# Gated linear recurrence into a gated MLP: squares, magnitude cap and scaled v made a group ahead, weights loaded in nine pieces

## The chip, the cores and the metric

One core of one Trainium2 chip runs the whole kernel. The metric is the device time of one execution in microseconds (us), as the median of several runs. TensorE is called PE below, VectorE DVE, ScalarE ACT, GpSimd POOL and SyncE SP.

## The reference, cut to what matters

Attention with a decaying complex state (batch 4, 8 heads, 768 steps, head size 48), then a gated MLP over 3072 tokens (384 to 1536 and back):

```python
mag = np.sqrt(a_re * a_re + a_im * a_im)
scale = np.minimum(mag, 0.999) / (mag + 1e-06)
a_re_n, a_im_n = (a_re * scale, a_im * scale)
for t in range(S):
    new_re = ar * S_re - ai * S_im
    new_im = ar * S_im + ai * S_re
    S_re, S_im = (new_re + k_t[:, None] * v_t[None, :], new_im)
    y[:, :, t] = einsum('bhd,bhde->bhe', q[:, :, t], S_re)
...
gate = 1.0 / (1.0 + np.exp(-(x @ w_gate)))
val = x @ w_val
return (gate * val @ w_out)
```

## The kernel before, in words

The 3072 tokens are 24 slabs of 128 (4 batches of 6 chunks). Slabs are gathered in ten groups of 1, 2, 3, 3, 3, 3, 3, 3, 2, 1 slabs, numbered 0 to 9. The recurrence is done in chunks: the logarithm of the magnitude and the phase of `a` are summed along the 128 steps by matmuls with triangular matrices, q and k are scaled and turned by the results, and a masked score matrix plus a carried state gives y.

For a group g these pieces exist:

- `loads_a(g)` and `loads_q(g)` issue on SP the loads of a_re and a_im (tile `a2`, 2 buffers) and of q, k (tile `qk`, 2 buffers) and v (tile `v32`, 1 buffer).
- `prep_a(g)`: ACT loads a table set with Ln and Exp, squares `a2` into `sq` (L162). POOL adds the two squares into `lm` (L165) and caps it (L167), slab by slab. ACT takes Ln of a_re (L170) and Exp of its negative (L171), both in place, then Ln of `lm` (L173). POOL multiplies a_im by 1/a_re (L175). Then for each slab PE sums `lm` (tile `cl`, L182), ACT makes exp(+cl/2) and exp(-cl/2) (tile `ee`, L183 and L185), SP sends the last row through DRAM (`scr`, `rbe`), POOL multiplies q and k by `ee` (L197) and makes the scaled 16-bit copy `v16` of v (L199).
- `prep_b(g)`: ACT loads a table set, takes Arctan of `a2` (L209), loads a third set (L210). For each slab PE sums the phase (tile `ct`, L215, L218, L231), POOL keeps the running phase (`run`, L223, L225), DVE rounds (L229), ACT takes Abs and two Sines (L235 to L238), DVE writes the turned k and q (`kst`, `qst`, L242).
- `attn(g)`: transposes (L292, L293), carried state (L268, L274, L278, L282), scores (L304), mask (L308), y (L319, L321), its copy by ACT (L324) and transpose (L331).
- `gateval(g)`: 12 blocks of the MLP's gate and value products on PE (L362, L367), Tanh on ACT (L370), the product on DVE (L371). Four PSUM buffers serve this and the output product.
- `outproj(g)`: the output product on PE (L381), a copy on ACT (L387) and the store.

The pieces are generators, and iteration i of the main loop has two halves. The first half merges the first two fifths of attn(i), outproj(i-2) and prep_a(i+1); the second merges the rest of attn(i), gateval(i-1) and prep_b(i+1). `merge` takes always the generator whose next step has the smallest share (step number divided by its count of steps). ACT runs its instructions in exactly this written order. PE, DVE, POOL and SP get their orders from a planner, which goes by program order among the instructions that its own model holds ready; each engine then runs its queue in order. A tile's next write waits until the old readers of its buffer are done.

The weights are loaded by 18 transfers on POOL's queue with a cast to 16 bit (6 of 128 rows by 1536 for gate and value, 12 of 128 by 384 for the output), issued behind the first group's L175.

Of the kernel before, what the change touches and what calls it, by code (L numbers as in the profile page):

```python
# [9 lines left out]
FT = mybir.ActivationFunctionType  # L10
ALU = mybir.AluOpType
# [6 lines left out]
YSC = 2.0**10  # L18
# [4 lines left out]
def kernel(  # L23
# [12 lines left out]
    nc = tc.nc  # L36
# [5 lines left out]
    DFF = moe_w_gate.shape[1]  # L42
    NFB = DFF // 128
# [5 lines left out]
    GROUPS = [SLABS[f:f + n] for f, n in zip(FIRST, SIZES)]  # L49
    NG = len(GROUPS)  # L50
# [41 lines left out]
    gs = [Grp() for _ in range(NG)]  # L92

    def loads_a(g):
        G = gs[g]
        G.a2 = pa.tile([L, 2, NS, HD], F32, name=f"a2_{g}", tag="a2")
        for s, (b, c) in enumerate(GROUPS[g]):
            for i, src in enumerate((a_re, a_im)):
                nc.sync.dma_start(
                    G.a2[:, i, s].rearrange("t (h d) -> t h d", d=D),  # L100
                    src[b, :, c * L:(c + 1) * L].rearrange("h t d -> t h d"))

    def loads_q(g):
        G = gs[g]
        G.qk = pq.tile([L, 2, NS, HD], F32, name=f"qk_{g}", tag="qk")
        G.v32 = pv_.tile([L, NS, HD], F32, name=f"v32_{g}", tag="v32", bufs=1)
        G.v16 = pv_.tile([L, NS, HD], F16, name=f"v16_{g}", tag="v16")
        for s, (b, c) in enumerate(GROUPS[g]):
            for dst, src in ((G.qk[:, 0, s], q), (G.qk[:, 1, s], k),
                             (G.v32[:, s], v)):  # L110
                nc.sync.dma_start(
                    dst.rearrange("t (h d) -> t h d", d=D),
                    src[b, :, c * L:(c + 1) * L].rearrange("h t d -> t h d"))
# [21 lines left out]
    wg16 = const.tile([128, 3, DFF], F16, name="wg16")  # L135
    wv16 = const.tile([128, 3, DFF], F16, name="wv16")
    wo16 = const.tile([128, NFB, DM], F16, name="wo16")

    def load_weights():
        for j in range(3):  # L140
            nc.gpsimd.dma_start(wg16[:, j], moe_w_gate[j * 128:(j + 1) * 128])
            nc.gpsimd.dma_start(wv16[:, j], moe_w_val[j * 128:(j + 1) * 128])
        for j in range(NFB):
            nc.gpsimd.dma_start(wo16[:, j], moe_w_out[j * 128:(j + 1) * 128])

    rbe, arr = {}, {}
    for b in range(B):
# [3 lines left out]
    scr = [dram.tile([NCH, HD], F32, name=f"scr{b}", bufs=1, tag=f"scr{b}")  # L151
           for b in range(B)]

    def prep_a(g):
        G = gs[g]
        n = len(GROUPS[g])
        ar, ai = G.a2[:, 0, :n], G.a2[:, 1, :n]
        G.lm = pa.tile([L, NS, HD], F32, name=f"lm_{g}", tag="lm")
        sq = pa.tile([L, 2, NS, HD], F32, name=f"sq_{g}", tag="sq", bufs=1)
        lm = G.lm[:, :n]  # L160
        nc.scalar.preload_act_table_set("natural_log_exp_and_others")  # L161
        nc.scalar.activation(out=sq[:, :, :n], in_=G.a2[:, :, :n],  # L162
                             func=FT.Square)
        for s in range(n):
            nc.gpsimd.tensor_tensor(out=G.lm[:, s], in0=sq[:, 0, s],  # L165
                                    in1=sq[:, 1, s], op=ALU.add)
            nc.gpsimd.tensor_scalar(out=G.lm[:, s], in0=G.lm[:, s],  # L167
                                    scalar1=CAP, scalar2=-1.0,
                                    op0=ALU.min, op1=ALU.max)
        nc.scalar.activation(out=ar, in_=ar, func=FT.Ln)  # L170
        nc.scalar.activation(out=ar, in_=ar, func=FT.Exp, scale=-1.0)  # L171
        yield
        nc.scalar.activation(out=lm, in_=lm, func=FT.Ln)  # L173
        for s in range(n):
            G.last_pool = nc.gpsimd.tensor_tensor(  # L175
                out=G.a2[:, 1, s], in0=G.a2[:, 1, s], in1=G.a2[:, 0, s],
                op=ALU.mult)
        yield
        for s, (b, c) in enumerate(GROUPS[g]):
            ee = pe_.tile([L, 2, HD], F32, name=f"ee_{g}_{s}", tag="ee")  # L180
            cl = ps_gen.tile([L, HD], F32, name=f"cl_{g}_{s}", tag="gen")
            nc.tensor.matmul(cl, wl_t, G.lm[:, s], start=True, stop=True)  # L182
            nc.scalar.activation(out=ee[:, 0], in_=cl, func=FT.Exp,  # L183
                                 scale=0.5)
            nc.scalar.activation(out=ee[:, 1], in_=cl, func=FT.Exp,  # L185
                                 scale=-0.5)
            nc.sync.dma_start(scr[b][c:c + 1], ee[L - 1:L, 0])
            with nc.allow_non_contiguous_dma(reason="column of decays"):
                for p0 in (0, 64):
                    nc.sync.dma_start(  # L190
                        rbe[b][p0:p0 + D, c],
                        scr[b][c].rearrange("(h d) -> d h", d=D))
            if c > 0:
                nc.vector.tensor_tensor(
                    out=arr[b][:, c - 1], in0=rbe[b][:, c - 1],
                    in1=rbe[b][:, c], op=ALU.mult)
            nc.gpsimd.tensor_tensor(out=G.qk[:, :, s], in0=G.qk[:, :, s],  # L197
                                    in1=ee, op=ALU.mult)
            nc.gpsimd.tensor_scalar(out=G.v16[:, s], in0=G.v32[:, s],  # L199
                                    scalar1=YSC, scalar2=1.0,  # L200
                                    op0=ALU.mult, op1=ALU.mult)
            yield

    def prep_b(g):
# [171 lines left out]
    def outproj(g):  # L376
        G = gs[g]
        for s, (b, c) in enumerate(GROUPS[g]):
            po = ps_moe.tile([128, DM], F32, name=f"po{g}_{s}", tag="moe")
            for fb in range(NFB):  # L380
                nc.tensor.matmul(po, G.p[:, fb, s * L:(s + 1) * L],  # L381
                                 wo16[:, fb], start=(fb == 0),
                                 stop=(fb == NFB - 1))
                if fb % 4 == 3 and fb < NFB - 1:
                    yield
            ot = pmoe.tile([128, DM], F32, name=f"ot{g}_{s}", tag="ot")
            nc.scalar.activation(out=ot, in_=po, func=FT.Copy, scale=0.5)  # L387
            nc.sync.dma_start(out[b * S + c * L:b * S + (c + 1) * L], ot)
            yield

    def merge(*streams):
        live = [[it, 0, n] for it, n in streams]
        while live:
            live.sort(key=lambda x: (x[1] + 1) / x[2])
            x = live[0]
            try:
                next(x[0])
                x[1] += 1
            except StopIteration:
                live.pop(0)  # L400

    def take(it, n):
        for _ in range(n):
            yield next(it)

    def run_all(it):
        for _ in it:
            pass

    def sz(g):  # L410
        return len(GROUPS[g])

    with tc.manual_schedule(engines={ACT}):
        loads_a(1)
        run_all(prep_a(0))
        with tc.issue_after(gs[0].last_pool.ins):
            load_weights()
        loads_q(1)
        run_all(prep_b(0))
        for i in range(NG + 2):  # L420
            st = []
            if i < NG:
                at = attn(i)
                na = 7 * sz(i)
                n1 = na * 2 // 5
                st.append((take(at, n1), n1))
            if 0 <= i - 2:
                st.append((outproj(i - 2), 3 * sz(i - 2)))
            if i + 1 < NG:
                if i + 2 < NG:  # L430
                    loads_a(i + 2)
                st.append((prep_a(i + 1), 2 + sz(i + 1)))
            merge(*st)
            st = []
            if i < NG:
                st.append((at, na - n1))
            if 0 <= i - 1 < NG:
                st.append((gateval(i - 1), 2 * NFB))
            if i + 1 < NG:
                if i + 2 < NG:  # L440
                    loads_q(i + 2)
                st.append((prep_b(i + 1), 1 + 2 * sz(i + 1)))
            merge(*st)
# [1 line left out]
_INS = ['q', 'k', 'v', 'a_re', 'a_im', 'moe_w_gate', 'moe_w_val', 'moe_w_out']  # L445
# [26 lines left out]
```

## Time and profile before

| what | value |
|---|---|
| device time, median of 3 runs | 370.19 us (368.79 to 371.55) |
| device time of the profiled execution | 373.35 us |
| its span, first to last instruction | 371.3 us |
| mean granted TensorE clock | 0.931 |
| PE busy | 277.8 us (75%) |
| PE weight loads | 181.4 us (49%) |
| ACT busy | 224.0 us (60%) |
| DVE busy | 206.1 us (55%) |
| POOL busy | 157.7 us (42%) |

Busy shares are of the span. The profiled execution lies 2.05 us above its span and 3.16 us above the median. No engine is busy all the time; the three rows of ACT, DVE and POOL say nothing of who waits for whom. ACT's load of the Ln and Exp table set (L161) is written once for each group, so its starts mark the iterations: iteration i begins where group i+1's is loaded.

### The profile page before, as it was taken

To read this page: it belongs to the slowest core of one execution; us is meant where nothing else is said; L and a number is where in the kernel's file an instruction comes from. 1 tells how busy PE (TensorE), PEld (TensorE's weight loads), DVE (VectorE), ACT (ScalarE), POOL (GpSimd) and SP (SyncE) were. 2 spreads that over 40 slices of the span, in tenths; PEclk is the share of its full clock that TensorE was granted. 3 is DMA by queue.
4 is the path that set the end of the run, shared out by engine and by line. 5 is a ranking of instruction groups with operands and counts; after the bars stand their busy time and mean duration, and the time that the engine had idled before them with its cause. 6 is when DMAs were issued, how large, how long until landed. Compare 5 with 4: busy or idle time off the path is not lost.

```text
span 371.3 us, 6375 instructions
## 1 busy us (share of the span) xinstructions
PE 277.8 (75%) x2328; PEld 181.4 (49%) x2328; DVE 206.1 (55%) x385; ACT 224.0 (60%) x376; POOL 157.7 (42%) x186
## 2 busy tenths in 40 slices
PE   0310753595569937997889967996799899999996
PEld 0100532364347614664556644663556566666774
DVE  1120281288068905695449725891588489667533
ACT  3604583848385748456774848674956684785343
POOL 3746719723771287026830485028700741320000
PEclk9999995899589968899889989998999999999999
DMA  7999999598166854149240943073202310100101
GB/s 147 199 197 176 185 129 151 71 146 148 33 101 104 147 107 70 39 84 163 56 85 15 187 100 66 3 132 83 44 2 44 102 7 0 51 18 0 65 23 42
DMA packets 150990, 32.70 MB, mean 88 GB/s; under 512 B 145048, under 2 KB 150192, under 8 KB 150960
## 3 DMA queue, kind: packets, MB, share of 16 engines
q1 hardware_dynamic: 148368, 28.76, 44.2%
q0 software_dynamic: 2592, 3.54, 5.3%
q8 instruction: 18, 0.29, 0.3%
q14 instruction: 12, 0.10, 0.1%
HBM read 31.07 MB, written 4.76 MB: 96 GB/s over the span
## 4 chain that ended last, share of the span: by engine, by line
PE 42%; ACT 21%; POOL 11%; DVE 9%; DMA 8%; issue 5%; SPq 3%; ACTq 0%; DVEq 0%; POOLq 0%
PE pg L362 8%; PE cl L182 8%; PE pv L367 7%; POOL lm L165 5%; PE ct L215 4%; PE po L381 3%; ACT sq L162 3%; POOL lm L167 3%; ACT lm L173 3%; DMA wv<-in_moe_w_val_dram 3%; DVE qst L242 2%; PE sc L304 2%; PE ct L218 2%; ACT L161 2%; ACT L208 2%
## 5 line engine op out<-in xcount | busy, mean ns | idle before, releaser
L182 PE MATMUL cl<-lm,wl_t 128*128 128x384 f32 x48 | 30.5, 737 | 60.3 <-ACT lm L173 60.3
L370 ACT ACTIVATE g<-pg 128x384 f16<-128x384 f32 (+2 forms) x120 | 49.5, 427 | 41.8 <-PE pg L362 35.5
L362 PE MATMUL pg<-xt,wg 128*128 128x384 f16 (+2 forms) x360 | 67.6, 296 | 7.6 <-ACT g L370 7.3
L367 PE MATMUL pv<-xt,wv 128*128 128x384 f16 (+2 forms) x360 | 68.8, 295 | 1.9 <-DVE p L371 1.1
L371 DVE SCALAR_TENSOR_TENSOR p<-g,pv 128x384 f16<-128x384 f16 (+2 forms) x120 | 54.8, 468 | 23.8 <-ACT g L370 19.5
L308 DVE TENSOR_TENSOR mst<-sc,msk_t 128x512 f16<-128x512 f32 x48 | 32.4, 682 | 46.3 <-PE sc L304 46.3
L381 PE MATMUL po<-wo,p 128*128 128x384 f16 x288 | 53.6, 326 | 0.0
L296 DVE COPY qkT<-tp 128x1024 f16<-128x1024 f16 x48 | 32.1, 684 | 38.6 <-PE tp L293 38.4
L197 POOL TENSOR_TENSOR qk<-qk,ee 128x768 f32<-128x768 f32 x24 | 44.3, 1859 | 11.9 <-ACT ee L185 11.0
L199 POOL TENSOR_SCALAR v<-v 128x384 f16<-128x384 f32 x24 | 13.4, 560 | 82.8 <-PE y L321 66.7
L165 POOL TENSOR_TENSOR lm<-sq 128x384 f32<-128x384 f32 x24 | 25.8, 1089 | 41.1 <-ACT sq L162 40.6
L362 PEld LDWEIGHTS <-wg 128*128 128x128 f16 x360 | 31.8, 99 | 22.2 <-issue 12.2
L182 PEld LDWEIGHTS cl<-lm,wl_t 128*128 128x128 f32 x48 | 10.5, 265 | 64.4 <-ACT lm L173 63.2
L367 PEld LDWEIGHTS <-wv 128*128 128x128 f16 x360 | 32.4, 98 | 17.9 <-issue 5.9
L215 PE MATMUL ct<-a,wt_t 128*128 128x384 f32 x48 | 25.0, 607 | 12.8 <-ACT a L209 12.8
L229 DVE TENSOR_SCALAR r<-ct 128x384 f16<-128x384 f32 x24 | 13.2, 551 | 37.1 <-PE ct L215 20.2
L381 PEld LDWEIGHTS <-p 128*128 128x128 f16 x288 | 26.3, 98 | 13.7 <-issue 0.2
L292 PE MATMUL tp<-idn_t,kst 128*128 128x128 f16 x192 | 30.6, 236 | 2.8 <-DVE kst L242 2.8
L293 PE MATMUL tp<-idn_t,qst 128*128 128x128 f16 x192 | 30.1, 235 | 1.2 <-DVE qst L242 1.2
L242 DVE TENSOR_TENSOR kst<-qk,cs 128x768 f16<-128x768 f32 x24 | 23.1, 960 | 7.9 <-ACT cs L238 5.4
L162 ACT ACTIVATE sq<-a 128x2304 f32<-128x2304 f32 (+2 forms) x10 | 17.4, 1740 | 14.7 <-DMA a<-in_a_im_dram 14.6
L292 PEld LDWEIGHTS <-kst 128*128 128x128 f16 x192 | 20.3, 107 | 8.1 <-DVE kst L242 4.8
(53 smaller groups left out, 506.1 us busy)
## 6 DMA issues: line engine op xcount, KB each, us to landing
a<-in_a_re_dram SPq DMA_DIRECT2D x24, 192.0 KB, 2.9
a<-in_a_im_dram SPq DMA_DIRECT2D x24, 192.0 KB, 4.2
qk<-in_q_dram SPq DMA_DIRECT2D x24, 192.0 KB, 3.3
qk<-in_k_dram SPq DMA_DIRECT2D x24, 192.0 KB, 3.9
v<-in_v_dram SPq DMA_DIRECT2D x24, 192.0 KB, 2.8
out_dram<-ot SPq DMA_DIRECT2D x24, 192.0 KB
wg<-in_moe_w_gate_dram POOLq DMA_DIRECT2D x3, 384.0 KB, 7.9
wv<-in_moe_w_val_dram POOLq DMA_DIRECT2D x3, 384.0 KB, 7.2
```

The costliest lines, as they stand in the source:

```text
L165: nc.gpsimd.tensor_tensor(out=G.lm[:, s], in0=sq[:, 0, s], in1=sq[:, 1, s], op=ALU.add)
L182: nc.tensor.matmul(cl, wl_t, G.lm[:, s], start=True, stop=True)
L197: nc.gpsimd.tensor_tensor(out=G.qk[:, :, s], in0=G.qk[:, :, s], in1=ee, op=ALU.mult)
L215: nc.tensor.matmul(ct, wt_t, th[:, s], start=True, stop=False, skip_group_check=True)
L292: nc.tensor.transpose(tp[:, 4 + i], G.ks[s][:, h], idn_t)
L296: nc.vector.tensor_copy(out=qkT, in_=tp)
L308: nc.vector.tensor_tensor(out=mst, in0=sc, in1=msk_t.unsqueeze(1).broadcast_to([L, 4, L]), op=ALU.mult)
L362: nc.tensor.matmul(pg, wg16[:, j, fc], G.xt[:, j, :nt], start=(j == 0), stop=(j == 2))
L367: nc.tensor.matmul(pv, wv16[:, j, fc], G.xt[:, j, :nt], start=(j == 0), stop=(j == 2))
L370: nc.scalar.activation(out=g16, in_=pg, func=FT.Tanh, scale=0.5)
L371: nc.vector.scalar_tensor_tensor(out=G.p[:, fb, :nt], in0=g16, scalar=1.0, op0=ALU.add, in1=pv, op1=ALU.mult)
L381: nc.tensor.matmul(po, G.p[:, fb, s * L:(s + 1) * L], wo16[:, fb], start=(fb == 0), stop=(fb == NFB - 1))
```

## The change: what it does, and the diff

Square, the two-square sum, the cap and the scaled copy of v leave prep_a and become a generator of their own, `prep_0`. For group i+2 it is merged into the second half of iteration i, beside attn(i), gateval(i-1) and prep_b(i+1). prep_a(i+1) begins with the table load and then takes Ln of a_re, Ln of `lm` and Exp in that order; it has one step fewer. Both loads of group i+2 stand at the start of iteration i (the loads of q, k and v stood between the halves). Before the main loop prep_0 runs for groups 0 and 1, and both loads of group 1 are written behind prep_a(0). The weights come in 9 transfers: 6 of 512 columns over all 384 rows, 3 of 512 rows of the output weights.

```diff
     def load_weights():
-        for j in range(3):
-            nc.gpsimd.dma_start(wg16[:, j], moe_w_gate[j * 128:(j + 1) * 128])
-            nc.gpsimd.dma_start(wv16[:, j], moe_w_val[j * 128:(j + 1) * 128])
-        for j in range(NFB):
-            nc.gpsimd.dma_start(wo16[:, j], moe_w_out[j * 128:(j + 1) * 128])
+        for f in range(0, DFF, 512):
+            for dst, src in ((wg16, moe_w_gate), (wv16, moe_w_val)):
+                nc.gpsimd.dma_start(
+                    dst[:, :, f:f + 512],
+                    src[:, f:f + 512].rearrange("(j p) f -> p j f", p=128))
+        for j in range(0, NFB, 4):
+            nc.gpsimd.dma_start(
+                wo16[:, j:j + 4],
+                moe_w_out[j * 128:(j + 4) * 128].rearrange(
+                    "(j p) f -> p j f", p=128))
...
-    def prep_a(g):
+    def prep_0(g):
         G = gs[g]
         n = len(GROUPS[g])
-        ar, ai = G.a2[:, 0, :n], G.a2[:, 1, :n]
         G.lm = pa.tile([L, NS, HD], F32, name=f"lm_{g}", tag="lm")
         sq = pa.tile([L, 2, NS, HD], F32, name=f"sq_{g}", tag="sq", bufs=1)
-        lm = G.lm[:, :n]
-        nc.scalar.preload_act_table_set("natural_log_exp_and_others")
         nc.scalar.activation(out=sq[:, :, :n], in_=G.a2[:, :, :n],
                              func=FT.Square)
         for s in range(n):
@@
             nc.gpsimd.tensor_scalar(out=G.lm[:, s], in0=G.lm[:, s],
                                     scalar1=CAP, scalar2=-1.0,
                                     op0=ALU.min, op1=ALU.max)
+            yield
+        for s in range(n):
+            nc.gpsimd.tensor_scalar(out=G.v16[:, s], in0=G.v32[:, s],
+                                    scalar1=YSC, scalar2=1.0,
+                                    op0=ALU.mult, op1=ALU.mult)
+        yield
+
+    def prep_a(g):
+        G = gs[g]
+        n = len(GROUPS[g])
+        ar, ai = G.a2[:, 0, :n], G.a2[:, 1, :n]
+        lm = G.lm[:, :n]
+        nc.scalar.preload_act_table_set("natural_log_exp_and_others")
         nc.scalar.activation(out=ar, in_=ar, func=FT.Ln)
+        nc.scalar.activation(out=lm, in_=lm, func=FT.Ln)
         nc.scalar.activation(out=ar, in_=ar, func=FT.Exp, scale=-1.0)
-        yield
-        nc.scalar.activation(out=lm, in_=lm, func=FT.Ln)
         for s in range(n):
@@
             nc.gpsimd.tensor_tensor(out=G.qk[:, :, s], in0=G.qk[:, :, s],
                                     in1=ee, op=ALU.mult)
-            nc.gpsimd.tensor_scalar(out=G.v16[:, s], in0=G.v32[:, s],
-                                    scalar1=YSC, scalar2=1.0,
-                                    op0=ALU.mult, op1=ALU.mult)
             yield
...
     with tc.manual_schedule(engines={ACT}):
+        run_all(prep_0(0))
+        run_all(prep_a(0))
         loads_a(1)
-        run_all(prep_a(0))
+        loads_q(1)
         with tc.issue_after(gs[0].last_pool.ins):
             load_weights()
-        loads_q(1)
         run_all(prep_b(0))
+        run_all(prep_0(1))
         for i in range(NG + 2):
             st = []
+            if i + 2 < NG:
+                loads_a(i + 2)
+                loads_q(i + 2)
...
             if i + 1 < NG:
-                if i + 2 < NG:
-                    loads_a(i + 2)
-                st.append((prep_a(i + 1), 2 + sz(i + 1)))
+                st.append((prep_a(i + 1), 1 + sz(i + 1)))
...
             if i + 1 < NG:
-                if i + 2 < NG:
-                    loads_q(i + 2)
                 st.append((prep_b(i + 1), 1 + 2 * sz(i + 1)))
+            if i + 2 < NG:
+                st.append((prep_0(i + 2), 1 + sz(i + 2)))
             merge(*st)
```

## Rows read from the trace of the kernel before

**Rows 1.** Waits of the whole execution: who waited for whom, us, times, longest.
```profile
PE cl L182 <- ACT lm L173: 60.3, 10, 15.6
...
ACT lm L173 <- POOL lm L167: 23.9, 10, 3.5
```

**Rows 2.** Timeline of ACT through iteration 5: start, duration, instruction, idle time before it.
```profile
207.24 1.28 ACT L161 ACT_TABLE_LOAD   x1
208.53 2.12 ACT L162 ACTIVATE sq<-a 128x2304 f32<-128x2304 f32 x1
210.69 1.17 ACT L170 ACTIVATE a<-a 128x1152 f32<-128x1152 f32 x1
...
216.34 1.16 ACT L173 ACTIVATE lm<-lm 128x1152 f32<-128x1152 f32 x1 [2.91 <-POOL lm L167]
218.51 0.49 ACT L183 ACTIVATE ee<-cl 128x384 f32<-128x384 f32 x1 [1.00 <-PE cl L182]
...
226.88 1.16 ACT L209 ACTIVATE a<-a 128x1152 f32<-128x1152 f32 x1
...
230.58 0.49 ACT L370 ACTIVATE g<-pg 128x384 f16<-128x384 f32 x1 [0.35 <-PE pg L362]
```

**Rows 3.** Timeline of POOL around iteration 5, and its last L199.
```profile
210.74 2.29 POOL L165 TENSOR_TENSOR lm<-sq 128x384 f32<-128x384 f32 x2 [3.91 <-ACT sq L162]
213.11 1.09 POOL L167 TENSOR_SCALAR lm<-lm 128x384 f32<-128x384 f32 x2
214.28 0.99 POOL L165 TENSOR_TENSOR lm<-sq 128x384 f32<-128x384 f32 x1
...
283.28 0.51 POOL L199 TENSOR_SCALAR v<-v 128x384 f16<-128x384 f32 x1 [13.31 <-PE y L321]
```

**Rows 4.** Stretches of iteration 5: length; busy PE, PEld, DVE, ACT, POOL; clock, DMA, GB/s.
```profile
207.20:214.10 6.90, 6.76 (x56) 4.01 (x53) 4.84 (x7) 6.14 (x6) 3.19 (x4) 1.00 0.99 175
214.10:217.50 3.40, 0.01 (x1) 0.00 (x0) 0.00 (x0) 1.16 (x1) 3.15 (x6) 1.00 0.53 124
217.50:223.00 5.50, 5.44 (x43) 3.85 (x44) 2.07 (x3) 3.00 (x9) 4.84 (x4) 0.69 0.34 72
223.00:228.10 5.10, 2.99 (x25) 1.59 (x20) 2.85 (x6) 5.03 (x7) 3.09 (x3) 1.00 0.63 103
228.10:246.40 18.30, 18.02 (x157) 11.69 (x158) 14.98 (x29) 10.98 (x24) 3.69 (x5) 1.00 0.26 47
```

**Rows 5.** The same columns for the whole iterations 1, 2 and 7.
```profile
51.20:88.10 36.90, 23.05 (x228) 16.34 (x229) 21.14 (x44) 23.40 (x40) 19.99 (x22) 0.81 0.92 140
88.10:127.70 39.60, 28.10 (x253) 20.31 (x251) 24.92 (x44) 24.16 (x41) 20.07 (x24) 0.83 0.56 96
...
285.40:318.90 33.50, 31.06 (x284) 19.90 (x283) 25.89 (x44) 22.66 (x39) 12.85 (x13) 1.00 0.14 31
```

**Rows 6.** Timeline of DVE: L268 beside an idle POOL, then beside L165.
```profile
89.14 0.55 DVE L268 TENSOR_TENSOR u<-P,arr 128x384 f32<-128x384 f32 x1
...
90.79 0.86 DVE L268 TENSOR_TENSOR u<-P,arr 128x384 f32<-128x384 f32 x1
```

**Rows 7.** Timeline of the start, and SP's last load of a in iteration 5.
```profile
27.83 0.53 POOL L144 DMA_DIRECT2D wo<-in_moe_w_out_dram x1 [0.18 <-issue]
30.73 1.48 ACT L162 ACTIVATE sq<-a 128x1536 f32<-128x1536 f32 x1 [11.60 <-DMA a<-in_a_im_dram]
36.35 2.93 PE L182 MATMUL cl<-lm,wl_t 128*128 128x384 f32 x4 [15.62 <-ACT lm L173]
41.97 1.00 SPq L99 DMA_DIRECT2D a<-in_a_im_dram  x1
47.92 0.49 ACT L235 ACTIVATE cs<-ct 128x384 f32<-128x384 f32 x1 [4.28 <-PE ct L231]
...
206.86 0.98 SPq L99 DMA_DIRECT2D a<-in_a_im_dram  x1
```

**Rows 8.** DMA issues: median time from issue to landing.
```profile
a<-in_a_im_dram SPq DMA_DIRECT2D x24, 192.0 KB, 4.2
```

## The prediction

> **What bounds the kernel now.** I read the waits of the whole execution first. PE stood 60.3 us before L182, the sum of `lm`, all of it for ACT's Ln of `lm`; ACT in turn stood 23.9 us before that Ln for POOL's cap [rows 1]. Ten waits each: one per group. So the next view is one iteration in order of time, and I take iteration 5, which lies far from the loads of the start.
>
> On ACT [rows 2]: table load at 207.24, Square of 2.12 us, Ln and Exp of a_re of 1.17 us each, an idle 2.91 us, Ln of `lm` from 216.34 to 217.50. On POOL [rows 3]: the three adds and caps run from 210.74, when Square is done, to about 216.3 and carry that idle time. PE shows the same in the table of stretches [rows 4]: full until 214.1, nothing for 3.4 us, then 5.5 us at a mean clock of 0.69 (between the two levels of 2.4 and 1.2 GHz, just behind the idle stretch), then 2.1 us more idle in 223.0 to 228.1 (2.99 busy of 5.10) until Arctan is through, then 18.30 us with 18.02 busy. So an iteration has a first half of 20.9 us that the chain Square, add, cap, Ln, `cl`, `ee`, Arctan sets, and a second half of 18.3 us that PE sets, with DVE behind it (14.98 busy) and ACT idle for 18.30 - 10.98 = 7.3 us. The page's shares (PE 75%, ACT 60%) hide this split.
>
> **What leaves the first half.** Square goes: 2.12 us. With `lm` capped long before, the wait of 2.91 us goes. ACT also stood 1.00 us before the first `ee` for `cl` [rows 2]; Exp, of 1.17 us, now stands behind Ln of `lm` and fills that. Sum 6.0 us on ACT. Does PE follow? Its idle time is 3.4 + 2.1 = 5.5 us, and the 5.5 us at clock 0.69 hold about 5.5 x 0.31 = 1.7 us of slowness: 7.2 us [rows 4]. ACT's 6.0 is the smaller and I take it. Next late is PE: `cl` is free about 3.6 us behind 207.24 (table 1.28, two Ln of 1.17), while PE has work until 214.1, so PE's wait there is gone and not shortened. If the planner puts `cl` at the very head of PE's queue, PE waits up to those 3.6 us again, which is the low end of this term: 6.0 - 3.6 = 2.4. POOL's multiply (L175) starts behind Exp, some 4.9 us into the iteration; it started 9.2 us in, behind the last cap at 216.3. It is not late.
>
> **What comes into the second half.** Its place follows from the merge: prep_0's first of four steps is due at 1/4, with the 6th of gateval's 24. Square then stands behind the third Tanh, where ACT was at 230.58 [rows 2]. It holds up the Tanh, y copies and Sines behind it for 2.12 us. PE waits for a Tanh only through the four PSUM buffers, two blocks later, and ACT has 7.3 us of idle time to catch up [rows 4]. Bounds 0 and 2.1; I take 0.7, since the idle time is spread in pieces. Its own input is not late: the last load of `a2` was issued at 206.86 [rows 7] and the median landing is 4.2 us [rows 8], so about 211, against some 224 for Square in the shortened iteration. Without these 13 us ACT would stand with Tanh behind it.
>
> POOL gets three adds (0.99 alone, 2.29 for the first two) and three caps (1.09 for two) there, about 5 us [rows 3]; it was busy 3.69 us of the 18.30 [rows 4]. The casts of the carried state queue behind one add at most. The price is on DVE: L268 took 0.55 us beside an idle POOL and 0.86 beside L165 [rows 6]. Some seven DVE instructions with two SBUF inputs (six L242, one L268) lie in this half. Two collisions of 0.3 make 0.6, which I take; bounds 0 and 4.6 (every one of the six POOL instructions stops DVE for its length, 3 x 0.99 + 3 x 0.55). The Trainium skill speaks against the move here (SBUF — State Buffer, section "Summary: rules for kernel authors"): a DVE instruction with two SBUF inputs and a GpSimd one that reads SBUF exclude each other, and the later waits for the whole of the earlier. The trace agrees in kind with its 0.86 against 0.55; by the rule at its fullest the term would be the 4.6.
>
> The scaled copies of v cost and gain nothing: the planner already makes them a group ahead. The last L199, group 9's, ran at 283.28, before iteration 7, which prepares group 8, began at 285.4 [rows 3, 5]. They move from an iteration's end to its middle, where POOL is idle.
>
> The net of a full iteration is 6.0 - 0.7 - 0.6 = 4.7 us, with bounds 2.4 - 2.1 - 4.6 = -4.3 and 7.2.
>
> **The sum.** Iterations 1 to 6 prepare groups of three slabs: 6 x 4.7 = 28.2. Iteration 7 prepares two and PE is idle for only 33.50 - 31.06 = 2.4 us [rows 5]: 1.5 (0 to 2.4). Iteration 8 prepares one slab: 0. Iterations 1 and 2 ran at clocks of 0.81 and 0.83 against 0.96 to 1.00 late [rows 5]; where the idle stretch before `cl` goes, some of that comes back beyond what one iteration 5 shows. PE's 28.10 busy us in iteration 2 at 0.83 hold up to 28.10 x 0.17 = 4.8 us; I take 1.5 for each of these two, 3 together (0 to 8).
>
> The start: group 1's Square waited until 30.73 for its loads, and PE idled 15.62 us before its `cl` [rows 7]. Three things change there. The table load moves behind that Square, 1.28 us beside POOL's 3 us of adds and caps: 0. Group 2's Square now stands in iteration 0's second half, ahead of the Abs and Sines that began at 47.92. Its last load was issued at 41.97 [rows 7], so by the median it lands near 46.2 and Square ends at 48.3, later if the DMA queue is full, as it is there: 1.5 lost (0 to 6). The loads of q, k and v are written earlier, but SP's queue is in order of readiness and waited for buffers there; behind them queue the decay rows and the output stores, whose readers come half an iteration later: 0.
>
> The weights: 18 issues of 0.53 us on POOL [rows 7] become 9 of three or four times the rows. If an issue costs the same, 4.8 us; if it goes by rows, 6 x 1.6 + 3 x 2.1 = 16. Either is hidden while everything waits for group 1's loads until 30.73; the last issue began at 27.83 [rows 7]. What counts is whether those loads land earlier or later beside weights in other portions. No row shows it. Bounds: 10 of the 15.62 us gained, 3 lost; I take 0, as the bytes stay.
>
> Together 28.2 + 1.5 + 3 - 1.5 = 31.2. From the profiled execution's 373.35 that gives 342.2; from the median of 370.19, which lies 3.2 lower, 339.0. I predict 339.
>
> **Rivals.**
> A. The second half pays most of it: Square in full (2.1) and 2.0 of collisions leave 6.0 - 4.1 = 1.9 in each of six iterations. 11.4 + 1.5 + 1.5 - 1.5 = 12.9: 357. For it: PE busy 18.02 of 18.30 and DVE 14.98. Against: 7.3 us idle on ACT.
> B. Square needs a table load of its own. In the trace it ran under the Ln and Exp set, never under that of L210. One load before and one behind it, 2 x 1.28 [rows 2], for the eight groups 2 to 9: 20.5, so 359.5. The Trainium skill (ScalarE: Activation LUTs, section "Table sets: the hidden batching unit") says that cheap functions are in every set but does not list Square there; by that the time would be the 339, and no row shows it.
> C. Group 1's loads land earlier, since the weights' smaller portions give them more turns: 10 us of the 15.62 are gained on top: 329.
> D. Slower: the second half grows by more than the first shrinks. This decides from 6.0 us on (24.3 in place of 18.3). Its price is Square in full and every POOL instruction stopping DVE, 2.1 + 4.6 = 6.7: six iterations lose 0.7 each and the start 6, with nothing from the clock or from iteration 7: 370.2 + 4.2 + 6 = 380. For it: DVE has only 3.3 us free there. Against: ACT's 7.3, and a collision cost 0.3 and not 1.0.
> E. It doesn't do what it says: the adds stay late because the planner queues them on POOL behind prep_a's work. Then only Square's 2.12 leaves: 6 x (2.1 - 0.7) = 8, so 362. Against: POOL is idle for most of that half [rows 4].
>
> **How the numbers follow.** Forecast (331 to 348) 0.62, A 0.15, B 0.05, C 0.11, D 0.05, E 0.02. The range 327 to 357 takes in the forecast, C and nearly all of A, more than 0.8, and leaves B, D and E out. A measurement of this kernel can tell about 1% from no change. Every case but D ends more than 1% lower: faster 0.92 (a little of A, B and E ends nearer than that), same 0.03, slower 0.05.
>
> **What the changed profile would show.** Right: PE's wait before L182 falls from 60.3 to about 20, most of it in the start; the wait of Ln of `lm` for POOL falls from 23.9 to under 6; table loads to Arctan take some 14 us where they took 20.9; the second half stays within 18 to 20; L242 and L268 get slower by some tenths. Wrong: a second half of 22 or more, PE waiting for Tanh (A); loads of a table around Square (B); Square idle for loads of `a2` in any iteration but the first two; an early wait of PE before L182 with the output product queued behind it, which is the planner's order at work.

## The result, and the profile after

The changed kernel takes 339.5 us (median of 4 runs, 338.22 to 339.91) against 370.87 for the kernel before beside it: a ratio of 0.9155, 95% interval 0.9104 to 0.9205. The forecast was 339.0. The profiled execution took 339.80 with a span of 338.0. So the number is right. In the sum behind it, what a late iteration gives is nearly right (5.3 us on average over iterations 4 to 6, 4.7 in the sum), but iteration 1 came out 8.0 us worse than its share and iterations 2 to 6 together 7.5 us better, and the two errors cancel.

From the page of the changed kernel, the busy time and the granted clock in 40 slices:
```profile
span 338.0 us, 6365 instructions
...
PE 268.2 (79%) x2328; PEld 175.5 (52%) x2328; DVE 211.5 (63%) x385; ACT 221.9 (66%) x377; POOL 161.6 (48%) x177
...
PEclk9999559759796999999999999999999999999999
```
ACT, DVE and POOL are as busy as before to within 6 us (224.0, 206.1 and 157.7), so most of what went is idle time. A part is not: PE's busy time fell by 9.6 us from 277.8, because PE now does the same work at a higher granted clock (iteration 3 is shown further down). The waits, which answer to [rows 1]:
```profile
PE ct L226 <- ACT a L220: 23.9, 8, 15.1
...
ACT a L220 <- POOL a L189: 12.9, 1, 12.9
...
PE cl L196 <- DMA qk<-in_k_dram: 9.3, 1, 9.3
PE cl L196 <- ACT lm L186: 9.1, 5, 4.7
...
ACT lm L186 <- POOL lm L169: 3.1, 2, 2.0
```
PE's wait before the sum of `lm` fell from 60.3 us to 19.0 in the page's group (L196 now); the 9.3 of it that the view puts down to a load are the very first wait of the execution, which in the kernel before stood under ACT. Ln's wait for POOL fell from 23.9 to 3.1. New is the second row: one wait of 12.9 us of Arctan for POOL's multiply, and the 15.1 us of PE behind it.

Iteration 5 on ACT, against [rows 2]:
```profile
186.79 1.28 ACT L184 ACT_TABLE_LOAD   x1
188.09 1.17 ACT L185 ACTIVATE a<-a 128x1152 f32<-128x1152 f32 x1
189.16 1.15 ACT L186 ACTIVATE lm<-lm 128x1152 f32<-128x1152 f32 x1
190.21 1.15 ACT L187 ACTIVATE a<-a 128x1152 f32<-128x1152 f32 x1
...
191.64 0.48 ACT L197 ACTIVATE ee<-cl 128x384 f32<-128x384 f32 x1
...
200.81 1.16 ACT L220 ACTIVATE a<-a 128x1152 f32<-128x1152 f32 x1
...
204.04 2.13 ACT L164 ACTIVATE sq<-a 128x2304 f32<-128x2304 f32 x1
...
220.76 1.28 ACT L184 ACT_TABLE_LOAD   x1
```
Three passes without a gap, the first `ee` 4.9 us into the iteration where it came 11.3 in, Arctan done after 15.2 us where it took 20.8. Square stands behind the third Tanh of the second half, under the table set loaded at L221, with no load around it. The two stretches, against [rows 4]:
```profile
186.80:202.00 15.20, 13.46 (x118) 8.37 (x116) 9.44 (x16) 12.91 (x19) 9.44 (x8) 1.00 0.95 162
202.00:220.80 18.80, 18.20 (x157) 11.72 (x158) 15.39 (x29) 12.82 (x25) 9.40 (x11) 1.00 0.31 53
```
In the first half PE is busy 13.46 of 15.20 us at full clock (the stretch at 0.69 is gone). The second half grew by 0.5 us. POOL is busy 9.40 us of the second half, where it was 3.69. The table below counts every iteration in each trace from ACT's load of the Ln and Exp set to the next; "start" is where iteration 1 begins, the last column runs from iteration 8 to the span's end. Its rows for the kernel before and the changed kernel:

| us | start | it 1 | it 2 | it 3 | it 4 | it 5 | it 6 | it 7 | rest |
|---|---|---|---|---|---|---|---|---|---|
| before | 51.2 | 35.4 | 39.5 | 41.0 | 40.2 | 39.1 | 39.0 | 33.5 | 52.4 |
| after | 52.9 | 37.2 | 31.4 | 32.4 | 32.9 | 34.0 | 35.6 | 29.7 | 52.0 |

Start and iteration 1 lose 1.7 and 1.8 us, iterations 2 to 7 gain 36.3, the rest 0.4: 33.3 in the span. ([rows 5] divides iterations 1 and 2 at 88.10, where the table set is loaded at 86.61; the granted clocks of 0.81 and 0.83 hold either way.)

### The profile page after: what moved, and what is told of

It reads as the page before. It is cut to its first block, busy times and chain, and to the rows that moved or that the text cites. A ratio compares the mean times of both kernels' runs of the same rounds, so it can differ in the third digit from the quotient of the medians.

```text
span 338.0 us, 6365 instructions
## 1 busy us (share of the span) xinstructions
PE 268.2 (79%) x2328; PEld 175.5 (52%) x2328; DVE 211.5 (63%) x385; ACT 221.9 (66%) x377; POOL 161.6 (48%) x177
## 4 chain that ended last, share of the span: by engine, by line
PE 48%; ACT 19%; DMA 10%; DVE 7%; POOL 6%; issue 5%; SPq 3%; DVEq 0%; ACTq 0%; POOLq 0%
PE pg L373 10%; PE pv L378 9%; PE po L392 9%; DMA v<-in_v_dram 5%; PE cl L196 4%; PE ct L226 4%; DMA a<-in_a_im_dram 3%; POOL qk L211 3%; PE ct L229 3%; ACT sq L164 2%; ACT g L381 2%; PE tp L304 2%; PE tp L303 2%; DVE qst L253 2%; ACT L184 2%
## 5 line engine op out<-in xcount | busy, mean ns | idle before, releaser
L378 PE MATMUL pv<-xt,wv 128*128 128x384 f16 (+2 forms) x360 | 68.9, 297 | 3.6 <-DVE p L382 2.8
L382 DVE SCALAR_TENSOR_TENSOR p<-g,pv 128x384 f16<-128x384 f16 (+2 forms) x120 | 54.4, 467 | 20.8 <-ACT g L381 17.0
L392 PE MATMUL po<-wo,p 128*128 128x384 f16 x288 | 55.2, 326 | 0.0
L307 DVE COPY qkT<-tp 128x1024 f16<-128x1024 f16 x48 | 32.4, 687 | 33.6 <-PE tp L304 33.3
L211 POOL TENSOR_TENSOR qk<-qk,ee 128x768 f32<-128x768 f32 x24 | 43.6, 1837 | 2.8 <-ACT ee L199 2.6
L226 PE MATMUL ct<-a,wt_t 128*128 128x384 f32 x48 | 24.6, 599 | 24.0 <-ACT a L220 23.9
L378 PEld LDWEIGHTS <-wv 128*128 128x128 f16 x360 | 32.4, 98 | 19.1 <-issue 7.1
L196 PE MATMUL cl<-lm,wl_t 128*128 128x384 f32 x48 | 24.1, 593 | 19.0 <-DMA qk<-in_k_dram 9.3
L319 DVE TENSOR_TENSOR mst<-sc,msk_t 128x512 f16<-128x512 f32 x48 | 32.4, 684 | 8.3 <-PE sc L315 8.1
L189 POOL TENSOR_TENSOR a<-a 128x384 f32<-128x384 f32 x24 | 23.8, 1015 | 28.7 <-ACT a L187 28.6
L174 POOL TENSOR_SCALAR v<-v 128x384 f16<-128x384 f32 x24 | 15.5, 644 | 43.2 <-PE y L332 25.8
L303 PE MATMUL tp<-idn_t,kst 128*128 128x128 f16 x192 | 29.8, 230 | 2.9 <-DVE kst L253 2.9
L304 PE MATMUL tp<-idn_t,qst 128*128 128x128 f16 x192 | 29.2, 229 | 1.8 <-DVE qst L253 1.8
L285 POOL CAST x<-u 128x384 f16<-128x384 f32 x20 | 11.3, 569 | 33.9 <-DVE u L279 21.4
L253 DVE TENSOR_TENSOR qst<-qk,cs 128x768 f16<-128x768 f32 x24 | 26.8, 1119 | 0.0
```

The costliest lines, as they stand in the source:

```text
L226: nc.tensor.matmul(ct, wt_t, th[:, s], start=True, stop=False, skip_group_check=True)
L253: nc.vector.tensor_tensor(out=dst.rearrange("p h (r x) -> p h r x", r=2)[:, :, :, 0:D], in0=G.qk[:, 1 - i, s].rearrange("p (h d) -> p h d" ...
L303: nc.tensor.transpose(tp[:, 4 + i], G.ks[s][:, h], idn_t)
L304: nc.tensor.transpose(tp[:, i], G.qs[s][:, h], idn_t)
L307: nc.vector.tensor_copy(out=qkT, in_=tp)
L378: nc.tensor.matmul(pv, wv16[:, j, fc], G.xt[:, j, :nt], start=(j == 0), stop=(j == 2))
```

## The experiments

My theory: the gain is the shortened chain on ACT in the first half, from Square's length and from POOL's add and cap; weights, v's copies and early loads carry nothing of it. The rivals: the start or the weights carry part; the second half pays more or less than I said. The loss in iteration 1 needed a theory of its own. In diffs and rows `...` stands for lines not shown.

**e1, the weights alone.** The kernel before with the nine pieces.
```diff
-        for j in range(3):
-            nc.gpsimd.dma_start(wg16[:, j], moe_w_gate[j * 128:(j + 1) * 128])
...
+        for f in range(0, DFF, 512):
+            for dst, src in ((wg16, moe_w_gate), (wv16, moe_w_val)):
```


> The kernel before with the nine weight pieces as the only edit. My theory (the gain is the first half's chain of Square, add, cap; the weights are hidden): the time stays within 1% of before, 367 to 374 us, even if group 1's loads land earlier than the 30.7 us of before, because q, k and v of group 1 still fill the DMA queues. Rival (the start was the gain: the 11 us by which group 1's Square comes earlier in the changed kernel are kept): 358 to 364 us.

Measured 371.27 us, ratio 0.999 (0.9956 to 1.0024). Group 1's Square did come earlier:
```profile
24.57 1.48 ACT L167 ACTIVATE sq<-a 128x1536 f32<-128x1536 f32 x1 [5.65 <-DMA a<-in_a_im_dram]
```
That is 6.2 us before [rows 7], and it is worth nothing that the medians show. In the kernel before, the weights are hidden.

**e2, the squares alone.** The kernel before with Square, add and cap in a prep_0 that is merged a group ahead, and Ln, Ln, Exp; the scaled copy of v, the loads and the weights as before.
```diff
...
+            if i + 2 < NG:
+                st.append((prep_0(i + 2), 1 + sz(i + 2)))
```


> The kernel before with Square, add and cap moved a group ahead and the order Ln, Ln, Exp; v16 stays in prep_a, loads and weights as before. My theory: it holds all of the gain and lacks the two new waits of the start (POOL's scaled copy of v in front of the multiply, decay rows behind the loads on SP), so 334 to 340 us. Rival (the earlier loads or the weights carry a part): 345 to 355 us.

Measured 334.04 us, 0.8955 (0.8905 to 0.9004): all of the gain and 5.5 us more than the whole change. Something else in the change costs time.

**e3, v's copy put back** behind the multiply of q and k, everything else as changed.
```diff
...
             nc.gpsimd.tensor_tensor(out=G.qk[:, :, s], in0=G.qk[:, :, s],
                                     in1=ee, op=ALU.mult)
+            nc.gpsimd.tensor_scalar(out=G.v16[:, s], in0=G.v32[:, s],
+                                    scalar1=YSC, scalar2=1.0,
+                                    op0=ALU.mult, op1=ALU.mult)
             yield
```


> The changed kernel with the scaled copy of v back in prep_a. My theory: POOL's multiply for group 1 no longer stands behind a copy that waits 13 us for v, Arctan of group 1 moves from 43.6 to about 31, but DMA is full until then and the decay rows still come late, so the time falls by 1 to 4 us: 335.5 to 338.5 us. Rival (the wait for v sets the start): 6 to 10 us less, 330 to 333. Second rival (copies ahead matter in the steady iterations): slower, 342 to 346.

Measured 340.27 us, 0.9133 (0.9094 to 0.9173): a miss, and no test of what I meant. The planner put the copies of group 1 in front of the multiply again (the same wait of Arctan, 12.7 us). Moving the instruction in the program did not move it behind that multiply in POOL's queue.

**e4, the weights put back** to 18 pieces in the changed kernel (e1's diff reversed).

> The changed kernel with the 18 row-wise weight pieces. My theory: group 1's Square goes back to about 30 us from 19.9, but as POOL then waits for v until 37.8 anyhow, the time changes by less than 1%: 337 to 343 us. Rival (the earlier Square is kept in the time): 345 to 351 us.

Measured 338.23 us, 0.9082 (0.9041 to 0.9122): no difference that can be told from the changed kernel. Its trace has group 1's Square at 27.18, where the changed kernel has it at 19.88: those 7.3 us are lost again in either kernel. Arctan of group 1 hardly waits for POOL here, and then group 2's Square waits for its loads:
```profile
41.72 0.84 ACT L215 ACTIVATE a<-a 128x768 f32<-128x768 f32 x1 [1.71 <-POOL a L184]
...
47.67 2.12 ACT L159 ACTIVATE sq<-a 128x2304 f32<-128x2304 f32 x1 [3.81 <-DMA a<-in_a_im_dram]
```
Iteration 1 begins at 52.7, as in the changed kernel (52.9).

**e5, the q, k and v loads of group 2 late again**, between the halves of iteration 0, in the changed kernel.
```diff
-                loads_q(i + 2)
+                if i > 0:
+                    loads_q(i + 2)
...
+            if i == 0:
+                loads_q(2)
```


> The changed kernel with one edit: the loads of q, k and v of group 2 stand between the halves of iteration 0, as before, so that the decay rows of group 1 go ahead of them on SP. My theory (iteration 1 is long because those rows come some 10 us late and the state, its cast, y and Arctan queue behind them): iteration 1 shrinks from 37.2 to about 34, and the time falls by 2.5 to 5 us, to 334.5 to 337. Rival (DMA is full anyhow, the q loads then come late instead): within 1 us, 338.5 to 340.5.

Measured 340.24 us, 0.9138 (0.9101 to 0.9175). That is the rival's time. Iteration 1 did fall, from 37.2 to 31.4, more than I expected, but iteration 2 rose from 31.4 to 39.3 and took it back. In that iteration, on POOL and PE:
```profile
88.40 3.22 POOL L189 TENSOR_TENSOR a<-a 128x384 f32<-128x384 f32 x3 [8.63 <-ACT a L187]
91.58 1.79 POOL L211 TENSOR_TENSOR qk<-qk,ee 128x768 f32<-128x768 f32 x1
93.32 1.28 POOL L285 CAST x<-u 128x384 f16<-128x384 f32 x2
...
94.20 0.20 PE L330 MATMUL y<-x,qkT 128*128 128x48 f16 x1 [5.75 <-POOL x L285]
```
The cast of the carried state stands behind POOL's multiplies, PE waits 5.75 us for it with the sums of `lm` queued behind, and ACT's y copy stands in front of the next `ee`. It is a jam of the same kind as in iteration 1 of the changed kernel, one iteration later.

**e6, the squares ahead with nine weight pieces**, loads as before: e2 with e1's diff.

> Squares, add and cap ahead with the loads as before (the 334 us version), plus the nine weight pieces. In that version POOL's adds for group 1 stand 12.5 us behind the 18 weight issues; nine pieces free POOL by about 20 us. My theory: DMA is full, so the freed chain waits for q, k and v instead, and the time stays within 1%: 331 to 336. Rival (that wait is the start's bound): 5 to 10 us less, 324 to 329.

Measured 331.12 us, 0.8885 (0.8863 to 0.8907): the fastest version of the study. It lies 2.9 us under e2, though the intervals of the two still touch (0.8905 and 0.8907); in the traces iteration 1 takes 34.0 us in e2 and 31.4 in e6, so here the nine pieces seem not to be hidden whole. Against e3 it differs only in where the loads are written, and it is 9.1 us faster.

**e7, Square issued twice** in the changed kernel.
```diff
         nc.scalar.activation(out=sq[:, :, :n], in_=G.a2[:, :, :n],
                              func=FT.Square)
+        nc.scalar.activation(out=sq[:, :, :n], in_=G.a2[:, :, :n],
+                             func=FT.Square)
```


> The changed kernel with Square issued twice into the same tile, 2.1 us more on ACT in each second half. My theory (a third of a Square's length shows, since ACT has 7 us of idle time in pieces): 0.7 x 6 and a little for the small groups, 4 to 5 us more, 342 to 346. Rival (hidden whole): 339 to 341. Second rival (ACT's written order makes all of it late): 13 to 16 us more, 352 to 356.

Measured 342.64 us, 0.9207 (0.9183 to 0.9230): 3.1 more, under the 4 to 5 that I expected. Iterations 2 to 6 are together 3.2 us longer, 0.6 each: about 0.3 of a Square shows.

**e8, POOL's add issued twice** in the changed kernel.
```diff
             nc.gpsimd.tensor_tensor(out=G.lm[:, s], in0=sq[:, 0, s],
                                     in1=sq[:, 1, s], op=ALU.add)
+            nc.gpsimd.tensor_tensor(out=G.lm[:, s], in0=sq[:, 0, s],
+                                    in1=sq[:, 1, s], op=ALU.add)
```


> The changed kernel with POOL's add issued twice, 24 x 1.0 us more on POOL beside the second halves. My theory (two collisions of 0.3 us with DVE per six POOL instructions, so one more in each group): 0.3 to 0.5 x 8, 2 to 4 us more, 341 to 344. Rival by exclusion at its fullest (each added instruction stops DVE for its length): up to 24 us more, 355 to 363. Third: nothing, 338.5 to 340.5.

Measured 348.81 us, 0.9373 (0.9351 to 0.9395): 9.3 more, over my 2 to 4 and far under the 24. 5.1 of it is iteration 1 (42.3 against 37.2), where Ln of `lm` waits 5.70 us for POOL and waited 2.02 in the changed kernel. Iterations 2 to 6 are 0.5 to 1.3 us longer, 0.9 each, about 0.3 per added instruction of 1.0. DVE's two-input instructions get longer, by the lines of the two kernels, changed first:
```profile
L253 DVE TENSOR_TENSOR kst<-qk,cs 128x768 f16<-128x768 f32 x24 | 23.7, 988 | 5.4 <-ACT cs L249 4.9
L253 DVE TENSOR_TENSOR qst<-qk,cs 128x768 f16<-128x768 f32 x24 | 26.8, 1119 | 0.0
```
```profile
L255 DVE TENSOR_TENSOR qst<-qk,cs 128x768 f16<-128x768 f32 x24 | 29.4, 1224 | 0.0
L255 DVE TENSOR_TENSOR kst<-qk,cs 128x768 f16<-128x768 f32 x24 | 26.9, 1120 | 5.3 <-ACT cs L251 5.3
```
Together that is 0.24 us per slab, or 0.71 us in a group of three, near the 0.9 per iteration; no run separates it from other costs of the add. In the kernel before the means were 960 and 963 ns.

**e9, the start's loads put back, e10, the loop's loads put back**, each from e3, so that the two together are e6.
The first diff is e9's, the second e10's.
```diff
         run_all(prep_0(0))
-        run_all(prep_a(0))
         loads_a(1)
-        loads_q(1)
+        run_all(prep_a(0))
         with tc.issue_after(gs[0].last_pool.ins):
             load_weights()
+        loads_q(1)
```
```diff
             if i + 2 < NG:
                 loads_a(i + 2)
-                loads_q(i + 2)
...
+                if i + 2 < NG:
+                    loads_q(i + 2)
                 st.append((prep_b(i + 1), 1 + 2 * sz(i + 1)))
```

> The version with v16 in prep_a (340.3 us) with only the start's loads put back as before; inside the loop the loads of q, k and v stay early. My theory (the loss against the 331 us version is made by the loop's early loads, through POOL's order in iteration 1): 338 to 341 us, iteration 1 near 37. Rival (the start's order makes it): 330 to 333.

> The version with v16 in prep_a (340.3 us) with only the loop's loads of q, k and v put back between the halves; the start stays as in the changed kernel. My theory: 330 to 333 us, iteration 1 near 31.5. Rival (the start's order makes the loss): 338 to 341.

Measured e9 337.05 us, 0.9069 (0.9035 to 0.9103), and e10 333.15 us, 0.8946 (0.8904 to 0.8988). From e3's 340.27 the loop's order is worth 7.1 us and the start's 3.2. Both times lie nearer to my theory than to the rival, each just outside the range that I gave, since the start's order carries a part too. In e9 iteration 1 is still 37.9 us long, as in e3; in e10 it is 29.9. There SP sends group 1's decay rows early, and DVE scales the state 5.4 us into iteration 1:
```profile
43.78 0.74 SPq L197 DMA_DIRECT2D scr<-ee  x2
```
```profile
58.28 0.54 DVE L278 TENSOR_TENSOR u<-P,arr 128x384 f32<-128x384 f32 x1
```

**e11, the cast of the carried state on DVE** in the changed kernel.
```diff
-                nc.gpsimd.tensor_copy(out=X[s], in_=u)
+                nc.vector.tensor_copy(out=X[s], in_=u)
```


> The changed kernel with the cast of the carried state (L285) on DVE in place of POOL, so that it can't stand behind POOL's multiplies of q and k. My theory (this queueing is what makes iteration 1 long): iteration 1 falls from 37.2 to 33 or less, the others gain or lose some tenths by DVE's 20 x 0.35 us: 332 to 336 us. Rival (the decay rows themselves come too late, whoever casts): 338 to 342.

Measured 338.85 us, 0.9115 (0.9077 to 0.9152): the rival's number. Iteration 1 fell only from 37.2 to 35.5. DVE there:
```profile
63.34 0.88 DVE L208 TENSOR_TENSOR arr<-rbe 128x8 f32<-128x8 f32 x1
64.26 0.56 DVE L279 TENSOR_TENSOR u<-P,arr 128x384 f32<-128x384 f32 x1
...
66.60 0.69 DVE L285 CAST x<-u 128x384 f16<-128x384 f32 x1
```
The first product of decays starts 11.0 us into the iteration, whoever casts. So taking the cast off POOL gives back 1.7 us, and the rows still come late. It is a lower bound: the cast still starts 1.8 us behind the end of the scaling, now in DVE's queue.

**e12, POOL's add and cap left out** of the kernel before.
```diff
-        for s in range(n):
-            nc.gpsimd.tensor_tensor(out=G.lm[:, s], in0=sq[:, 0, s],
-                                    in1=sq[:, 1, s], op=ALU.add)
-            nc.gpsimd.tensor_scalar(out=G.lm[:, s], in0=G.lm[:, s],
-                                    scalar1=CAP, scalar2=-1.0,
-                                    op0=ALU.min, op1=ALU.max)
...
-        nc.scalar.activation(out=lm, in_=lm, func=FT.Ln)
+        nc.scalar.activation(out=lm, in_=sq[:, 0, :n], func=FT.Ln)
```


> The kernel before without POOL's add and cap: Ln reads the square of a_re directly, so the magnitude lacks a_im and the cap; Square stays in the first half. This prices POOL's share of the chain alone. My theory: 2.9 us of ACT's wait for POOL in each full iteration plus some of the clock, 6 x 3.3 and 3 for the rest: 346 to 352 us. Rival (Square's length on ACT is what counted): above 358. Second rival (PE's idle time was POOL's alone, Square's place is free): 338 to 343.

Measured 345.00 us, 0.926 (0.9211 to 0.9309), a little under the expectation and above the second rival. Iteration 5, against [rows 4], in its two halves:
```profile
189.98:206.30 16.32, 13.70 (x118) 8.34 (x116) 10.11 (x16) 15.05 (x19) 9.54 (x8) 1.00 0.84 151
206.30:224.60 18.30, 17.98 (x157) 11.68 (x158) 14.98 (x29) 11.00 (x23) 3.69 (x5) 1.00 0.31 52
```
With Square still in place the first half falls from 20.9 to 16.3 us, and the stretch at a clock of 0.69 is gone. The table of the runs that bear on the split:

| us | start | it 1 | it 2 | it 3 | it 4 | it 5 | it 6 | it 7 | rest |
|---|---|---|---|---|---|---|---|---|---|
| e12, Square in place, POOL's part left out | 50.9 | 31.7 | 35.9 | 37.4 | 34.1 | 34.6 | 34.5 | 32.1 | 52.0 |
| e6, squares and weights | 50.7 | 31.4 | 31.3 | 31.7 | 33.2 | 34.0 | 35.2 | 29.7 | 52.0 |
| e5, group 2's loads late | 52.3 | 31.4 | 39.3 | 32.6 | 32.9 | 34.0 | 35.6 | 29.7 | 52.0 |
| e9, start as before | 50.4 | 37.9 | 30.3 | 32.0 | 32.9 | 34.0 | 35.6 | 29.7 | 52.0 |
| e10, loop as before | 52.9 | 29.9 | 32.2 | 33.3 | 33.2 | 34.0 | 35.6 | 29.7 | 52.0 |

Iterations 2 to 7 sum to 232.3 us before, 208.7 in e12, 195.2 in e6. POOL's part of the chain, left out, is worth 23.6 us; moving Square as well, with Exp behind Ln of `lm`, and paying for all in the second half, another 13.5. The two shares differ by iteration. In iterations 4 to 6 POOL's part alone gives 15.0 of the 15.9 us that e6 gains; in 2, 3 and 7 it gives 8.6 of 21.2.

## Why the prediction was right, step by step

**What leaves the first half** (6.0 us: Square 2.12, the wait for POOL 2.91, 1.0 before `ee`): the total is shown, the split is not as I had it. In iterations 4 to 6 Arctan's pass ends 5.7, 5.6 and 5.2 us earlier in the iteration. In e12 it ends 4.6, 4.5 and 4.5 earlier: POOL's part is worth that much and not 2.91, and Square with the wait before `ee` 0.8 to 1.1 and not 3.1. From the start of Ln of `lm` to the end of Arctan's pass iteration 5 took 11.7 us before, at a clock of 0.69 in the middle, and takes 10.2 in e12 at full clock; the difference is near the slowness of 1.7 that I had worked out and then left out of the sum. Why Square's place gives so little more there is not tested.

In iterations 2 and 3 Arctan's pass ends 9.4 and 8.6 us earlier, more than the term. PE had stood idle for 8.0 and 6.3 us before L182 (3.5 in iteration 5), at mean clocks of 0.83 and 0.88. Iteration 3, before and changed:
```profile
126.06:167.09 41.03, 32.05 (x253) 20.03 (x251) 24.51 (x45) 25.79 (x41) 18.22 (x20) 0.88 0.47 82
```
```profile
121.47:153.86 32.39, 29.16 (x254) 18.18 (x250) 24.92 (x45) 25.17 (x41) 20.57 (x23) 1.00 0.75 124
```
Of its 8.6 us, 5.7 are PE's idle time and 2.9 are the same matmuls at a higher clock. I had put 3 us of clock on iterations 1 and 2 and none on 3; iteration 5 was the wrong one to scale the early ones from. My reading is that in these two iterations the output product of one or two slabs leaves PE less to do while ACT's chain runs; no run tests it.

**What comes into the second half** (1.3 us: Square 0.7, collisions 0.6): 18.30 became 18.8 in iteration 5; over iterations 2 to 6 the second halves change by +1.4, 0.0, -1.5, +0.5 and +1.8, +0.4 on average. The prices of one more piece are 0.6 for another Square (e7), where I took 0.7, and 0.9 for three more adds (e8), where I took 0.6 for three adds and three caps. POOL itself in iteration 5:
```profile
208.27 1.72 POOL L169 TENSOR_SCALAR lm<-lm 128x384 f32<-128x384 f32 x2
210.05 1.60 POOL L167 TENSOR_TENSOR lm<-sq 128x384 f32<-128x384 f32 x1
```
Caps of 1.72 for two and an add of 1.60, where [rows 3] has 1.09 and 0.99: POOL's instructions get longer too, and not DVE's alone. Rival A (each iteration keeps only 1.9) and rival D (the second half pays more than 6.0) are out by the same numbers.

**Iteration 7** gave 3.8 where I took 1.5, all in its first half (16.2 to 12.3). PE's idle time of 2.4 us was not the limit, since work moved: by the two traces PE does 259 matmuls in iteration 7 where it did 285, and 300 in iteration 6 where it did 274. So part of what iteration 7 gains iteration 6 pays; the two together gave 7.2 where the sum has 6.2.

**"The loads of q, k and v are written earlier ... whose readers come half an iteration later: 0."** This step failed. The start of the changed kernel, on ACT, POOL and SP:
```profile
19.88 1.48 ACT L164 ACTIVATE sq<-a 128x1536 f32<-128x1536 f32 x1 [1.98 <-DMA a<-in_a_im_dram]
...
37.84 0.51 POOL L174 TENSOR_SCALAR v<-v 128x384 f16<-128x384 f32 x1 [13.28 <-DMA v<-in_v_dram]
...
41.60 1.94 POOL L189 TENSOR_TENSOR a<-a 128x384 f32<-128x384 f32 x2
43.58 0.84 ACT L220 ACTIVATE a<-a 128x768 f32<-128x768 f32 x1 [12.95 <-POOL a L189]
...
47.37 2.12 ACT L164 ACTIVATE sq<-a 128x2304 f32<-128x2304 f32 x1 [1.64 <-DMA a<-in_a_im_dram]
...
53.23 0.74 SPq L201 DMA_DIRECT2D scr<-ee  x2
...
55.94 2.45 SPq L204 DMA_DIRECT2D rbe<-scr  x4
```
Two queues were passed, and the second cost. On POOL the copies of v stand in front of the multiply and wait 13.28 us for v, though in the kernel before the multiply went first. It is not their place in the program that does it: e3, e6, e9 and e10 have the copies back in prep_a and the same order in the queue. On SP nine loads of group 2 stand in front of group 1's decay rows: made at 27 to 29 us, sent at 53.23, where the kernel before sent them at 43.07. Their reader did come half an iteration later, but the rows pass through two transfers, one behind the other (`scr`, then `rbe`), and in iteration 1 they were late:
```profile
64.36 0.56 DVE L279 TENSOR_TENSOR u<-P,arr 128x384 f32<-128x384 f32 x1
...
65.37 3.56 POOL L211 TENSOR_TENSOR qk<-qk,ee 128x768 f32<-128x768 f32 x2
68.88 1.28 POOL L285 CAST x<-u 128x384 f16<-128x384 f32 x2
...
69.76 0.20 PE L330 MATMUL y<-x,qkT 128*128 128x48 f16 x1 [2.92 <-POOL x L285]
...
70.60 0.49 ACT L335 ACTIVATE y<-y 128x384 f16<-128x384 f32 x1 [4.53 <-PE y L332]
```
The state is scaled at 64.4, its cast waits for POOL until 68.9, then PE, then ACT's y copy with Arctan written behind it. In e6, with the loads as before, the same cast runs at 57.03, ahead of POOL's multiplies:
```profile
57.03 0.50 POOL L284 CAST x<-u 128x384 f16<-128x384 f32 x1 [1.36 <-DVE u L278]
57.50 3.23 POOL L185 TENSOR_TENSOR a<-a 128x384 f32<-128x384 f32 x3
```
The loss in iteration 1 is shown to come from the loop's early loads (e10 against e3). That it passes by the decay rows and by the cast behind them is what the traces show: the state is scaled 11.5 us into iteration 1 in the changed kernel and 5.4 in e10. How the loss divides between the two I can only bound, at least 1.7 us for the cast (e11). So the term that I put at nothing cost 7.1 us in the loop (e10 against e3), and 9.1 with the start's order (e6 against e3).

**The start** (1.5 us lost): 1.7, by the means forecast. Group 2's Square starts at 47.37, when its loads have landed (my estimate was 46.2), and the Abs and Sines stand behind it. The wait for v ahead of it does not set the time: in e4 Arctan is done 1.9 us earlier, Square then idles 3.81 us for the same loads, and iteration 1 begins at 52.7 all the same. In e6 and e9, with the start's loads as before, Square starts at 45.65 and 45.27 and iteration 1 at 50.7 and 50.4, although Arctan waits 11.6 us or more for POOL there. **Rival C** (group 1's loads land earlier, 10 us gained) happened in its first half and not in its second: group 1's Square ran 10.9 us earlier and nothing was kept, since POOL's multiply stood behind the copies of v until 41.60 and iteration 1 waits for group 2's loads. e1 and e4 show the same from both sides. **Rival B** (a table load for Square) is out: of ten Squares only the first, ahead of any other ACT work, has a load at its line. The Trainium skill (ScalarE: Activation LUTs, section "Table sets: the hidden batching unit") says that cheap functions are in every set; this trace agrees for Square, which its list does not name, as far as the set of L221 shows it. **Rival E** (the adds stay late) is out by Ln's wait of 3.1 us.

**The copies of v** cost nothing that shows in the loop, as I said (e3 has them back and takes 340.27 us). In the start they bring one wait of 13 us, which I did not see; by e4, e6 and e9 it sets nothing either.

So the sum closed by luck in part: 31.2 forecast, 33.3 in the span (31.4 by the medians); iterations 2 to 6 gave 32.5 where I had 25.0 for them (five at 4.7, and 1.5 of clock), iteration 7 2.3 more, and iteration 1 took 1.8 where I had it giving 6.2.

## What to carry to other kernels

A piece of work can be moved a group ahead nearly free when the stretch it moves into has a different limit; read the price from that stretch, and read the gain from several iterations, not from one. What is moved with it is priced by the queue: a load written earlier can go ahead of small transfers that a later step waits for, and an operation that waits for a load can stand ahead of one that was ready. The parts of a chain are not worth their lengths: without POOL's part alone, the late iterations had nearly all of the gain. Where a planner orders an engine, look at the order it made before crediting an edit; here the part of the change that "only" wrote loads earlier cost 9.1 us (e6 against e3), and leaving it out gave the fastest version (331.1 us).

## What the runs showed of the hardware

The weight issues on POOL:
```profile
14.84 0.82 POOL L142 DMA_DIRECT2D wg<-in_moe_w_gate_dram  x1
...
17.97 2.26 POOL L146 DMA_DIRECT2D wo<-in_moe_w_out_dram  x3
20.20 0.54 POOL L234 COPY run<-a 128x384 f32<-128x384 f32 x1
```
An issue of 384 or 512 rows took 0.75 to 0.82 us (the first 0.98) where one of 128 rows took 0.53 [rows 7]: neither of my two bounds (the same each, or by rows), and close to the lower. With nine in place of 18 POOL was free at 20.2 us, where its last issue began at 27.83; of the 18, four waited 0.9 to 1.6 us each for earlier weight transfers. An issue on SP took 0.43 us for most of the first ones and up to 5.88 us (a load of v at 19.36); what stands behind a long one is sent that much later. I take it that the queue was full there, but no row shows how full it was.
